# The second batch's first transform stage on pre-formed sums and differences, placed wholly ahead of the MLP

## The chip, the cores and the metric

The kernel runs on one core of a Trainium2 chip. The metric is the time of one execution in device microseconds; the table below gives it as the median of several runs. Engines are named as the profile names them: PE is TensorE (matrix products), PEld its weight loads, DVE is VectorE, ACT is ScalarE, POOL is GpSimd, SP is SyncE, which here only issues DMAs. SBUF is the on-chip working memory, PSUM the banks into which PE accumulates.

## What is computed

A Fourier filter over the sequence of 3008 tokens, then a two-layer MLP over all 24064 tokens.

```python
x: (8, 3008, 256)   w_r, w_i: (256, 256)   moe_w_in: (256, 2048)   moe_w_out: (2048, 256)

X = np.fft.rfft(x, axis=1)
Yr = Xr @ w_r - Xi @ w_i + b_r
Yi = Xr @ w_i + Xi @ w_r + b_i
Yr = np.sign(Yr) * np.maximum(np.abs(Yr) - 0.01, 0.0)      # and Yi likewise
y = np.fft.irfft(Yr + 1j * Yi, n=3008, axis=1)
...
h = y.reshape(24064, 256) @ w_in
out = np.maximum(0.01 * h, h) @ w_out
```

The MLP's weights arrive as float64 and are turned into pairs of floats (`hi` and `lo`) on the chip.

## The kernel before

**Tiling.** 3008 = 47 x 64. A batch's forward transform is a stage over 47 points (`stage_a`, with the constant matrices `fa`), a round trip of the result through HBM (`u_dram`), and a stage over 64 points (`stage_b`). Then come the products with `w_r` and `w_i` (`proj`), the threshold, the inverse stage over 64 points (`stage_g`), a second round trip (`v_dram`), and the inverse stage over 47 points (`inverse`), which makes token columns for the MLP. `fwd(b)` runs the first stage of batch b, `mid(b)` the middle ones, in 12 steps (`NPAIR`).

**The MLP** runs over 47 chunks of 512 tokens, in 8 steps each: `moe_a` and `moe_b` make the hidden layer in PSUM banks of the tag `psh` (four of them), ACT and DVE turn it into the pair `gh`, `gl`, and `moe_o` multiplies that by `w_out`.

**Batches.** Batches 0 and 1 go first: `fwd(0)`, then `mid(0)`, and inside the steps of `mid(0)` the reads of `x` for batch 1 (`fp`, lines 719 to 732). After `mid(0)` come `inverse` and `forms` for the first chunk of tokens, and the MLP starts. From there the other batches' stages are threaded through the MLP.

**First stage of batch 1** (`stage_a1`, line 273). The symmetric stage needs the sum and the difference of two halves of the input, xa and xb. For batch 0 DVE forms them (`fold`). For batch 1 nothing forms them: each of the two outputs takes two matrix products, one on xa and one on xb, so that a chunk of input costs four products instead of two; for this a third, negated matrix `fa2` is made by ACT (line 707). The input comes in seven chunks (six of 512 columns, one of 256). Five chunks run ahead of the MLP and two, numbers 4 and 5, inside its first steps (`if i in (2, 4): next(fp.gen)`), in banks of the tag `psf`.

**Order.** Instructions are put in order by a scheduler that works with the priorities in which the code is recorded; `tc.issue_after(...)` holds an instruction behind another one in that order. Each engine, and each engine's DMA queue, then runs its instructions strictly in that order, and waits on semaphores. SP issues nearly all reads, `u_dram<-xin` writes of batch 1 (line 283) and `vin<-v_dram` reads of the first inverse (line 461); ACT issues the `v_dram<-v` writes of `mid(0)` (line 420).

**Names and lines of before** that are used below: L282 ACT copies the first stage's result out of PSUM; L482 PE's products of `inverse`; L485, L486, L488, L495 the ACT and DVE work behind them; L507, L508 the casts of the token columns; L94 and L609 the products of the MLP; L133 to L139, L164 to L174, L202 to L204 the conversion of the weights; L349, L350 the two steps that make the tile `ef` of a step of `mid`; L382, L390, L391, L392 the DVE chain of one step behind `proj` (the bias, the sum, the clipping, the threshold); L396, L400 ACT's making of `zf`; L418 ACT's copy of `v`. In batches 1 to 7 L382 runs on POOL, for batch 0 on DVE.

Of the kernel before, what the change touches and what calls it, by code (L numbers as in the profile page):

```python
# [8 lines left out]
F32 = mybir.dt.float32  # L9
# [9 lines left out]
N1, N2, NK1 = 47, 64, 24  # L19
NG, NS = 5, 13  # L20
P = 128
PA = NK1 * NG
# [8 lines left out]
def spectral_mlp_kernel(  # L31
# [18 lines left out]
    D = w_r.shape[0]  # L50
# [3 lines left out]
    NPAIR = NK1 // 2  # L54
# [11 lines left out]
    sb = ctx.enter_context(tc.tile_pool(name="sb", bufs=2))  # L66
    dram = ctx.enter_context(tc.tile_pool(name="dram", bufs=2, space=bass.MemoryType.DRAM))
    ps = ctx.enter_context(tc.tile_pool(name="ps", bufs=1, space=bass.MemoryType.PSUM))
    sync, act, dve, pool = nc.sync, nc.scalar, nc.vector, nc.gpsimd

    def bank(tag, bufs):
        return ps.tile([P, 512], F32, name=tag, tag=tag, bufs=bufs)

    def products(dst, pairs):

        terms = []
        for l, r in pairs:
            terms += [(l[0], r[0]), (l[0], r[1]), (l[1], r[0])] if len(l) == 2 else [(l[0], r[0])]
        for i, (a, b) in enumerate(terms):
            last = nc.tensor.matmul(dst, a, b, start=(i == 0), stop=(i == len(terms) - 1))  # L80
        return last
# [18 lines left out]
    consts = {}  # L100
# [41 lines left out]
    made, converted, parted = [], [], []  # L142
# [67 lines left out]
    u_dram = {}  # L210
    v_dram = {}

    reads, written, turned, turning, thresholded = [], [], [], [], []
    NX = -(-NS // 2)
    XT = [("gf", 2)] + [("gl", 2)] * 2 + [("gh", 2)] * 2 + [("yc", 2)] * 2
    XT1 = [("yc", 2)] * 2 + [("gf", 2), ("gh", 2), ("yl", 2), ("yh", 2), ("gh", 2)]
# [1 line left out]
    def fwd(b):  # L218
        ud = dram.tile([2, NK1, NG * NS, D], F32, name="u_dram", tag="u_dram", bufs=NPRE + 1)
        u_dram[b] = ud  # L220
        uv = ud.rearrange("c k (g s) d -> c (k g) (s d)", g=NG)
        x_t, s_t = {}, {}

        def load(c):
            cols = slice(2 * c * D, min(2 * c + 2, NS) * D)
            n = cols.stop - cols.start
            if b < NPRE:
                tag, bufs = (XT, XT1)[b][c]
                x2 = sb.tile([PA, 2, 2 * D], F32, name="xin", tag=tag, bufs=bufs)
                x_t[c] = [x2[:, h, :n] for h in range(2)]  # L230
            else:
                x_t[c] = [
                    sb.tile([PA, 2 * D], F32, name=f"xin{h}", tag="uv"[h], bufs=3 - h)[:, :n] for h in range(2)
                ]
            for h, t in enumerate(x_t[c]):
                if b == 0:
                    (act if h else sync).dma_start(t, x[b, h, :, cols])
                else:
                    with tc.issue_after(reads[-1].ins):
                        sync.dma_start(t, x[b, h, :, cols])  # L240

        def fold(c):
            xa, xb = x_t[c]
            n = xa.shape[1]
            eng = dve
            xs = sb.tile([PA, 2 * D], F32, name="xs", tag="zf", bufs=1)[:, :n] if b else xs3[:, c % 3, :n]
            eng.tensor_add(xs, xa, xb)
            eng.tensor_sub(xa, xa, xb)
            s_t[c] = [(xs,), (xa,)] if b < NPRE else [xs, xa]

        def split(c, h):
            t = s_t[c][h]
            n = t.shape[1]
            z = sb.tile([PA, 2, 2 * D], F32R, name="xz", tag="ez"[h], bufs=1)
            xh, xl = z[:, 0, :n], z[:, 1, :n]
            dve.tensor_copy(xh, t)
            dve.tensor_sub(xl, t, xh.bitcast(F32))  # L257
            s_t[c][h] = (xh, xl)

        def stage_a(c, h):  # L260
            t = x_t[c][h]
            n = t.shape[1]
            pa = (bank("psf", 2) if b else bank("psh", 4))[:PA, :n]
            products(pa, [(consts[f"fa{h}"] if b else consts[f"fa{h}32"], s_t[c][h])])
            t = x_t[c][1 - h]
            cp = act.copy(t, pa)
            if b == 0:
                turned[:] = [cp]
            st = (act if b else sync).dma_start(uv[h, :, 2 * c * D:2 * c * D + n], t)
            if b == 0:  # L270
                written.append(st)

        def stage_a1(c):

            n = x_t[c][0].shape[1]
            pas = [(bank("psf", 2) if c in (4, 5) else bank("psh", 4))[:PA, :n] for _ in range(2)]
            for h in range(2):
                with tc.issue_after(turning[NPAIR - 2].ins):
                    products(pas[h], [
                        (consts[f"fa{h}32"], (x_t[c][0],)), (consts[f"fa{2 * h}32"], (x_t[c][1],))])  # L280
            for h in range(2):
                act.copy(x_t[c][h], pas[h])  # L282
                sync.dma_start(uv[h, :, 2 * c * D:2 * c * D + n], x_t[c][h])

        if b == 1:
            for c in range(NX):
                load(c)
                yield 0
            for c in (0, 1, 2, 3, 6, 4, 5):
                stage_a1(c)  # L290
                yield 6 * x_t[c][0].shape[1]
            return

        ahead = 2 if b >= NPRE else NX
        for c in range(ahead):
            load(c)
        yield 4 * CS if b >= NPRE else 0
        fold(0)
        if b >= NPRE:
            split(0, 0)  # L300
        yield 0
        for c in range(NX):
            for h in range(2):
                if h == 0 and c + ahead < NX:
                    load(c + ahead)
                if h == 0 and c + 1 < NX:
                    fold(c + 1)
                stage_a(c, h)
                if b >= NPRE and (c + h < NX):
                    split(c + h, 1 - h)  # L310
                yield 3 * x_t[c][h].shape[1]


    def mid(b):
        ud = u_dram[b]
        vd = dram.tile([2, NK1, NG * NS, D], F32, name="v_dram", tag="v_dram")
# [95 lines left out]
        def stage_g(j):  # L412
            pg = bank("psh", 4) if b < 1 else bank("psf", 2)
            last = products(pg, [(consts["gb" if b else "gb32"], tuple(flat(z) for z in z_t.pop(j)))])
            if b == 0:
                turning.append(last)
            v = sb.tile([P, 2, D], F32, name="v", tag="v" if b else "y")
            act.copy(flat(v), pg)  # L418
            for c in range(2):
                act.dma_start(vd[c, 2 * j:2 * j + 2, :N2, :].rearrange("k n d -> n k d"), v[c * N2:(c + 1) * N2])  # L420

        for j in range(2):
            load(j)
# [31 lines left out]
    def v_load(pi):  # L455
        vin = sb.tile([PA, 2, 2, D], F32, name="vin", tag="vin")
        (b, s, _), (b1, _, _) = pairs[pi]
        for c in range(2):
            if b == b1:
                vv = v_dram[b].rearrange("c k (g s) d -> c (k g) s d", g=NG)  # L460
                ld = sync.dma_start(vin[:, c, :, :], vv[c, :, s:s + 2, :])
                if pi < 2:
                    reads.append(ld)
                continue
            for i, (b_, s_, _) in enumerate(pairs[pi]):
                vv = v_dram[b_].rearrange("c k (g s) d -> c (k g) s d", g=NG)
                sync.dma_start(vin[:, c, i, :], vv[c, :, s_, :])
        v_t[pi] = vin
# [218 lines left out]
    fa32 = sb.tile([PA, 3, PA], F32, name="fa32", tag="xi", bufs=1)  # L687
    for h in range(2):
        sync.dma_start(fa32[:, h], fa[h])
    for h in range(3):  # L690
        consts[f"fa{h}32"] = (fa32[:, h],)
    xs3 = sb.tile([PA, 3, 2 * D], F32, name="xs3", tag="yl")
    f0 = Stream(fwd(0), FWD)
# [10 lines left out]
    win_tmp = (  # L704
        sb.tile([P, NH * NIN], F32, name="cva", tag="vin"), sb.tile([P, NH * NIN], F32, name="cvq", tag="gf"),
        sb.tile([P, 4, 2, P], F32, name="ws", tag="yh"))
    act.mul(fa32[:, 2], fa32[:, 1], -1.0)
    convert_win(0)
    with tc.issue_after(turned[0].ins):
        split_consts()  # L710
# [22 lines left out]
    m0.finish()  # L733
    with tc.issue_after(thresholded[-1].ins):
        convert_win(3)
    fp.to(0.69)
    for p in due[0]:
        v_load(p)
    for eh in range(NH):
        for p in due[0]:  # L740
            inverse(p, eh)
    for _ in forms(0):
        pass
    next(wout)
    next(wout)


    mids = [Stream(mid(b), MID + PAUSE) for b in range(1, NB)]
# [1 line left out]
    for i, pos in enumerate(moe()):  # L750
        if i % 2 == 0 and len(converted) < NQ:
            with tc.issue_after(made[0].ins), tc.issue_after(made[1].ins):
                next(wout, None)
        if i in (2, 4):
            with tc.issue_after(parted[0].ins), tc.issue_after(parted[1].ins):
                next(fp.gen)
        while cur + 1 < NB - 1 and pos >= (read[cur + 1] if cur >= 0 else 0):
            for s in streams:
                s.finish()
            cur += 1  # L760
            streams = ([Stream(fwd(cur + 1), FWD + 4 * CS)] if cur else []) + [mids[cur]]
        frac = (pos - read[cur]) / (read[cur + 1] - read[cur]) if cur + 1 < NB else 1
        if cur == 0:
            frac = max(0, frac - 0.2) * 1.25
        work = frac / 0.95 * sum(s.total for s in streams)
        with tc.issue_after(converted[-1].ins) if cur == 0 else nullcontext():
            for s in streams:
                s.to(work / s.total)
                work = max(0, work - s.total)
# [103 lines left out]
```

## Time and profile before

| | us |
|---|---|
| median of 3 runs | 2571.74 (2568.99 to 2573.2) |
| the profiled execution | 2568.88 |
| its span, first to last instruction | 2567.1 |
| busy: PE, DVE, ACT, POOL | 2527.2, 1882.8, 1677.5, 118.9 |
| end of `mid(0)` on PE (last product of `stage_g`) | about 100.5 |
| first product of the MLP | 120.17 |

The 1.8 us by which the profiled execution exceeds its span lie around the program. Times in the text are counted from the start of the span. In the profile's lists a line names the source line, the engine, the operation, the tile written and the tiles read, the shape, the count, and then busy time, the mean length of one, and the idle time before it with what ended it. A product of two fp32 operands appears as two records. A merged piece of a timeline has its start, its length, and its count.

### The profile page before, as it was taken

The numbers are of one execution on the slowest core, as the hardware profiler recorded it, in microseconds if no ns is written. First come the engines' busy times: TensorE is split into PE (matmuls) and PEld (weight loads), VectorE is DVE, ScalarE is ACT, GpSimd is POOL, SyncE is SP. The second block draws the span as 40 slices with busy tenths as digits, with TensorE's granted clock in tenths as the row PEclk, the third lists the DMA queues.
The fourth block names the chain that finished last, engine by engine and source line by source line (L and its number), as shares of the span: only waits on it lengthen the run. The fifth ranks groups of instructions, "written<-read, shape, count | busy, mean of one in ns | idle before, by whom it ended". The sixth has DMA issues, their size and how long they took to land.

```text
span 2567.1 us, 42449 instructions
## 1 busy us (share of the span) xinstructions
PE 2527.2 (98%) x16204; PEld 2269.8 (88%) x16204; DVE 1882.8 (73%) x3460; ACT 1677.5 (65%) x3151; POOL 118.9 (5%) x96
## 2 busy tenths in 40 slices
PE   6999999999999999999999999999999999999999
PEld 4689888999899998999989999899998998999998
DVE  7787777777877778777787677867768777666665
ACT  4776666677566765677666676567665676655564
POOL 0001000000000000000000000000000000000000
PEclk8999999999999999999999999999999999999999
DMA  8631133111321113111141111412114111100000
GB/s 267 176 93 50 42 91 88 41 50 45 103 67 46 50 37 112 59 49 49 42 113 53 50 49 38 120 54 58 34 38 132 46 54 41 44 21 29 9 17 17
DMA packets 119904, 165.12 MB, mean 64 GB/s; under 512 B 13597, under 2 KB 69909, under 8 KB 119701
## 3 DMA queue, kind: packets, MB, share of 16 engines
q1 hardware_dynamic: 79112, 115.54, 14.7%
q10 hardware_dynamic: 40589, 46.87, 7.1%
q8 instruction: 128, 2.10, 0.4%
q14 instruction: 75, 0.61, 0.1%
HBM read 86.60 MB, written 75.76 MB: 63 GB/s over the span
## 4 chain that ended last, share of the span: by engine, by line
PE 89%; DMA 4%; DVE 3%; ACT 2%; issue 1%; ACTq 0%; SPq 0%; DVEq 0%
PE pso L609 38%; PE psh L94 34%; PE psf L80 11%; PE psf L482 3%; PE psf L345 3%; DMA xin<-x_dram 1%; DMA u_dram<-xin 1%; PE psh L80 1%; DVE gl L562 1%; DMA v_dram<-v 0%; DMA u<-u_dram 0%; DVE xz L257 0%; DVE gf L593 0%; ACT zf L400 0%; DMA vin<-v_dram 0%
## 5 line engine op out<-in xcount | busy, mean ns | idle before, releaser
L94 PE MATMUL psh<-yh,win_hi 128*128 128x256 f32 (+1 forms) x2608 | 741.3, 285 | 2.1 <-DVE gf L593 2.0
L94 PE MATMUL psh<-yl,win_hi 128*128 128x256 f32 (+1 forms) x2608 | 732.3, 281 | 0.0
L94 PE MATMUL psh<-yh,win_lo 128*128 128x256 f32 (+1 forms) x2608 | 729.6, 281 | 0.0
L562 DVE TENSOR_TENSOR gl<-gf,gh 128x1024 fp32r<-128x1024 f32 x376 | 461.0, 1226 | 309.8 <-ACT gh L560 305.9
L609 PE MATMUL pso<-gl,wout_hi 128*128 128x512 f32 x1504 | 591.6, 393 | 1.1 <-DVE gl L562 1.1
L609 PE MATMUL pso<-gh,wout_hi 128*128 128x512 f32 x1504 | 591.1, 393 | 1.0 <-ACT gh L560 1.0
L609 PE MATMUL pso<-gh,wout_lo 128*128 128x512 f32 x1504 | 589.6, 392 | 0.0
L94 PEld LDWEIGHTS psh<-yh,win_hi 128*128 128x128 f32 x2608 | 489.9, 188 | 19.7 <-DVE gf L593 4.9
L94 PEld LDWEIGHTS psh<-yl,win_hi 128*128 128x128 f32 x2608 | 490.4, 188 | 17.4 <-issue 0.5
L94 PEld LDWEIGHTS psh<-yh,win_lo 128*128 128x128 f32 x2608 | 489.0, 188 | 2.1
L560 ACT CAST gh<-gf 128x1024 fp32r<-128x1024 f32 x376 | 395.3, 1051 | 44.4 <-PE pso L609 34.9
L596 ACT ACTIVATE gf<-gf 128x768 f32<-128x768 f32 x368 | 311.7, 847 | 150.4 <-DVE gf L593 139.4
L609 PEld LDWEIGHTS pso<-gl,wout_hi 128*128 128x128 f32 x1504 | 282.5, 188 | 61.4 <-DVE gl L562 2.9
L609 PEld LDWEIGHTS pso<-gh,wout_hi 128*128 128x128 f32 x1504 | 282.8, 188 | 47.3 <-ACT gh L560 1.8
L609 PEld LDWEIGHTS pso<-gh,wout_lo 128*128 128x128 f32 x1504 | 282.5, 188 | 46.5 <-issue 0.2
L595 ACT ACTIVATE gf<-psh 128x256 f32<-128x256 f32 x368 | 142.0, 386 | 239.1 <-PE psh L94 232.0
L593 DVE TENSOR_TENSOR gf<-psh,u 128x512 f32<-128x512 f32 x368 | 252.4, 686 | 34.4 <-PE psh L94 30.7
L577 ACT COPY p<-psh 128x256 f32<-128x256 f32 x368 | 137.0, 372 | 158.0 <-PE psh L94 149.6
L382 POOL TENSOR_TENSOR kb<-bias,kc 128x512 f32<-128x512 f32 x84 | 116.3, 1385 | 2074.3 <-ACT kc L380 1877.0
L578 DVE TENSOR_TENSOR u<-psh,p 128x256 f32<-128x256 f32 x368 | 154.6, 420 | 73.8 <-ACT p L577 72.6
L580 DVE TENSOR_TENSOR gf<-psh,u 128x256 f32<-128x256 f32 x368 | 154.8, 421 | 31.1 <-PE psh L94 17.2
L581 DVE TENSOR_TENSOR gf<-psh,gf 128x256 f32<-128x256 f32 x368 | 154.5, 420 | 5.5
(128 smaller groups left out, 3173.0 us busy)
## 6 DMA issues: line engine op xcount, KB each, us to landing
u<-u_dram SPq DMA_DIRECT2D x192, 128.0 KB, 2.8
v_dram<-v ACTq DMA_DIRECT2D x192, 128.0 KB, 2.4
out_dram<-ob SPq DMA_DIRECT2D x94, 256.0 KB, 2.0
vin<-v_dram SPq DMA_DIRECT2D x96, 240.0 KB, 3.6
xin<-x_dram SPq DMA_DIRECT2D x90, 240.0 KB, 3.0
u_dram<-xin ACTq DMA_DIRECT2D x72, 240.0 KB, 2.4
u_dram<-xin SPq DMA_DIRECT2D x24, 240.0 KB, 4.4
raw<-w_out_dram SPq DMA_DIRECT2D x8, 512.0 KB, 5.3
```

The lines of the kernel that those rows point to most:

```text
L80: last = nc.tensor.matmul(dst, a, b, start=(i == 0), stop=(i == len(terms) - 1))
L94: mlp[:] = [nc.tensor.matmul(dst, a, b, start=start and i == 0, stop=i == 2, skip_group_check=True)]
L560: cp = act.copy(gh, g)
L562: parted[:] = [cp, dve.tensor_sub(gl, g, gh.bitcast(F32))]
L577: act.copy(p1, b1[:, lo])
L578: dve.tensor_add(u2, b1[:, hi], p1)
L580: dve.tensor_add(g[:, 3], b2[:, hi], u2)
L581: dve.tensor_add(g[:, 3], b2[:, lo], g[:, 3])
L593: dve.tensor_add(g[:, 1:3], b2.rearrange("p (k n) -> p k n", k=2), u2.unsqueeze(1).broadcast_to([P, 2, HT]))
L595: act.activation(g[:, 0], b1[:, lo], AF.Prelu, alpha=SLOPE)
L596: act.activation(g[:, 1:4], g[:, 1:4], AF.Prelu, alpha=SLOPE)
L609: mlp[:] = [nc.tensor.matmul(po, a[:, f, s], r[:, i], start=(f == 0 and j == 0), stop=(f == NF - 1 and j == 2),)]
```

## The change

POOL now forms sum and difference of each chunk of batch 1 as soon as it is read (`fold1`): an add into a scratch tile, a subtraction in place, and a copy of the sum over xb. The scratch tile has one buffer, under the tag `t`, and the last `v` tile of `mid(0)` takes the same buffer. `stage_a1` then needs one product for each output, and the matrix `fa2` and its ACT instruction go. All seven chunks run ahead of the MLP: five ahead of the first `inverse`, the others between the first `inverse` calls. The reads of `v_dram` are put ahead of the writes of `u_dram` in SP's queue, and the conversion of the first two pieces of `w_out` is held behind the last `v_dram` write.

```diff
+        def fold1(c):
+
+            xa, xb = x_t[c]
+            t = sb.tile([PA, 2 * D], F32, name="xs", tag="t", bufs=1)[:, :xa.shape[1]]
+            pool.tensor_add(t, xa, xb)
+            pool.tensor_sub(xa, xa, xb)
+            pool.tensor_copy(xb, t)
+
...
-            pas = [(bank("psf", 2) if c in (4, 5) else bank("psh", 4))[:PA, :n] for _ in range(2)]
+            pas = [bank("psh", 4)[:PA, :n] for _ in range(2)]
             for h in range(2):
                 with tc.issue_after(turning[NPAIR - 2].ins):
-                    products(pas[h], [
-                        (consts[f"fa{h}32"], (x_t[c][0],)), (consts[f"fa{2 * h}32"], (x_t[c][1],))])
+                    filled[:] = [products(pas[h], [(consts[f"fa{h}32"], (x_t[c][1 - h],))])]
             for h in range(2):
                 act.copy(x_t[c][h], pas[h])
-                sync.dma_start(uv[h, :, 2 * c * D:2 * c * D + n], x_t[c][h])
+                with tc.issue_after(reads[-1].ins):
+                    sync.dma_start(uv[h, :, 2 * c * D:2 * c * D + n], x_t[c][h])
...
             for c in range(NX):
                 load(c)
+                fold1(c)
                 yield 0
-            for c in (0, 1, 2, 3, 6, 4, 5):
+            for c in range(NX):
                 stage_a1(c)
-                yield 6 * x_t[c][0].shape[1]
+                yield 0
...
-            v = sb.tile([P, 2, D], F32, name="v", tag="v" if b else "y")
+            v = sb.tile([P, 2, D], F32, name="v", tag="v" if b else "y") if b or j < NPAIR - 1 else sb.tile(
+                [P, 2, D], F32, name="v", tag="t", bufs=1)
...
-    act.mul(fa32[:, 2], fa32[:, 1], -1.0)
...
-    fp.to(0.69)
     for p in due[0]:
         v_load(p)
+    for _ in range(NX - 2):
+        next(fp.gen)
+    last = filled[0]
     for eh in range(NH):
         for p in due[0]:
-            inverse(p, eh)
+            with tc.issue_after(last.ins):
+                inverse(p, eh)
+            next(fp.gen, None)
     for _ in forms(0):
         pass
-    next(wout)
-    next(wout)
+    with tc.issue_after(returned[0].ins):
+        next(wout)
+        next(wout)
...
-        if i in (2, 4):
-            with tc.issue_after(parted[0].ins), tc.issue_after(parted[1].ins):
-                next(fp.gen)
```

On POOL, during `mid(0)`, there stood nothing between the zeroing of two tiles and the first bias sum of batch 1; `xs` is the scratch tile and `xin` a chunk of input, and after the change 21 instructions stand there, of which the first six are shown:

```order
L328 MEMSET zero 48x256 x2
L246 ISA
L246 TENSOR_TENSOR xs<-xin 120x512
L247 TENSOR_TENSOR xin<-xin 120x512
L248 COPY xin<-xs 120x512
L246 TENSOR_TENSOR xs<-xin 120x512
L247 TENSOR_TENSOR xin<-xin 120x512
L248 COPY xin<-xs 120x512
```

Each waits for the one before it on POOL. On PE, between the last product of `stage_g` (`psh<-zf`) and the first of the MLP (`psh<-yh`), the pieces of the first stage (`psh<-xin`) and of `inverse` (`psf<-ga,vin`) stood and stand so:

```order
 L80 MATMUL psh<-zf,w_105 128x512 x3
-L80 MATMUL psh<-xin,fa_66 120x512 x12
-L482 MATMUL psf<-ga,vin 128x128 x4
-L80 MATMUL psh<-xin,fa_66 120x512 x4
+L80 MATMUL psh<-xin,fa_66 120x512 x10
+L494 MATMUL psf<-ga,vin 128x128 x6
+L80 MATMUL psh<-xin,fa_66 120x512 x2
+L494 MATMUL psf<-ga,vin 128x128 x2
 L80 MATMUL psh<-xin,fa_66 120x256 x2
-L482 MATMUL psf<-ga,vin 128x128 x3
-L80 MATMUL psh<-xin,fa_66 120x256 x2
-L482 MATMUL psf<-ga,vin 128x128 x9
```

Sixteen products of 512 columns and four of 256 have become twelve and two there, and the eight of chunks 4 and 5 no longer stand in the MLP. On ACT, the end of the same stretch, from a first-stage copy of 256 columns (`xin<-psh`) to the MLP's first activation, stood and stands so (first before, then after the change):

```order
L282 COPY xin<-psh 120x256 x2
L485 COPY odd<-psf 128x240
L495 COPY yc<-y 128x42
L507 CAST yh<-yc 128x512
L495 COPY yc<-y 128x428
```

```order
L289 COPY xin<-psh 120x512 x2
L497 COPY odd<-psf 128x240
L289 COPY xin<-psh 120x256 x2
L202 CAST wout_hi<-cva 128x512
L507 COPY yc<-y 128x42
L507 COPY yc<-y 128x428
L497 COPY odd<-psf 128x240
L519 CAST yh<-yc 128x512
```

The copies of all seven chunks (14 instead of 10) and a cast of `w_out` now stand ahead of the first cast of token columns (`yh`).

More of the change, by code (lines that the diff above doesn't have):

```diff
@@ L211, in spectral_mlp_kernel @@
     v_dram = {}
-    reads, written, turned, turning, thresholded = [], [], [], [], []
+    reads, written, turned, turning, thresholded, filled, returned = [], [], [], [], [], [], []
     NX = -(-NS // 2)
@@ L416, in stage_g @@
                 turning.append(last)
-            v = sb.tile([P, 2, D], F32, name="v", tag="v" if b else "y")
+            v = sb.tile([P, 2, D], F32, name="v", tag="v" if b else "y") if b or j < NPAIR - 1 else sb.tile(
+                [P, 2, D], F32, name="v", tag="t", bufs=1)
             act.copy(flat(v), pg)
             for c in range(2):
-                act.dma_start(vd[c, 2 * j:2 * j + 2, :N2, :].rearrange("k n d -> n k d"), v[c * N2:(c + 1) * N2])
+                put = act.dma_start(vd[c, 2 * j:2 * j + 2, :N2, :].rearrange("k n d -> n k d"), v[c * N2:(c + 1) * N2])
+                if b == 0:
+                    returned[:] = [put]
         for j in range(2):
@@ L689, in spectral_mlp_kernel @@
         sync.dma_start(fa32[:, h], fa[h])
-    for h in range(3):
+    for h in range(2):
         consts[f"fa{h}32"] = (fa32[:, h],)
```

## The prediction

> **What bounds the kernel now.** I read the page first, then the busy time by stretches, since the shares are averages over unlike stages.
>
> ```profile
> PE 2527.2 (98%) x16204; PEld 2269.8 (88%) x16204; DVE 1882.8 (73%) x3460; ACT 1677.5 (65%) x3151; POOL 118.9 (5%) x96
> 65.20:86.40 21.20, 20.21 (x96) 15.67 (x97) 15.42 (x28) 17.88 (x34) 0.00 (x0) 1.00 0.74 203
> 86.40:98.10 11.70, 10.24 (x46) 7.45 (x44) 7.97 (x15) 8.87 (x18) 0.00 (x0) 1.00 0.29 67
> 101.40:124.40 23.00, 22.55 (x84) 13.00 (x83) 18.68 (x36) 15.44 (x32) 0.00 (x0) 1.00 0.83 250
> 120.10:170.00 49.90, 49.90 (x224) 38.70 (x224) 42.09 (x74) 36.56 (x67) 0.00 (x0) 1.00 0.36 108
> ```
>
> In a stretch's row stand its length, then the busy time of PE, PEld, DVE, ACT and POOL, the granted PE clock, and the DMA share with GB/s. From 120 us on PE has no gap, at full clock, so a product taken out of the MLP gives its whole time. Between the end of `mid(0)` and the MLP (101.4 to 124.4) PE is nearly full too, but DVE has 18.68 of 23.00 us and ACT 15.44. In `mid(0)` PE, ACT and DVE share the work (20.21, 17.88 and 15.42 of 21.20), in a chain from engine to engine. POOL is empty until then: what it is given there lies beside the others, unless it slows them.
>
> **PE's part.** The records of the first stage of batch 1, in PE's timeline (start, length, count) and by tile:
>
> ```profile
> L80 PE MATMUL psh<-xin,fa x40: 379/592/594, 100.5 to 117.3; 120*120 120x512 f32 x32, 120*120 120x256 f32 x8
> L80 PE MATMUL psf<-xin,fa x16: 590/592/594, 121.7 to 144.3; 120*120 120x512 f32 x16
> 100.54 10.46 PE L80 MATMUL psh<-xin,fa 120*120 120x512 f32 x24
> 111.74 4.46 PE L80 MATMUL psh<-xin,fa 120*120 120x512 f32 x12
> 121.66 3.60 PE L80 MATMUL psf<-xin,fa 120*120 120x512 f32 x8
> 124.69 0.80 PE L94 MATMUL psh<-yh,win_hi 128*128 128x512 f32 x1
> 137.14 1.88 PE L80 MATMUL psf<-xin,fa 120*120 120x512 f32 x4
> 143.00 1.88 PE L80 MATMUL psf<-xin,fa 120*120 120x512 f32 x4
> ```
>
> Twenty-four records take 10.46 us, of which the last has 0.59 (a modelled end): 9.87 / 23 = 0.43 us from one record of 512 columns to the next, and 0.86 for a product of two records. All 48 + 8 records make 24 x 0.86 + 4 x 0.43 = 22.4 us. Half of that, 11.2 us, goes. Three pieces must be told apart. The two at 137.14 and 143.00 lie inside the full MLP: 4 x 0.86 = **3.4 us** gained. The piece at 121.66 (3.4 us) and half of the products ahead of 120 (4.3 us) lie where the MLP's first chunk is still being made; there PE gains 7.7 us of room, but the stage ends sooner only as far as ACT and DVE let it.
>
> **ACT's part of that stage.** These are ACT's groups that wait there, or are added to, from 102.0 to 124.5.
>
> ```profile
> L282 ACT COPY xin<-psh 120x512 f32<-120x512 f32 x8 | 4.6, 586 | 2.4 <-PE psh L80 2.4
> L282 ACT COPY xin<-psh 120x256 f32<-120x256 f32 x2 | 0.7, 372 | 1.3 <-PE psh L80 1.2
> L495 ACT COPY yc<-y 128x470 f32<-128x470 f32 x2 | 1.2, 584 | 1.7 <-ACT odd L485 0.9 <-DVE y L488 0.8
> L133 ACT ACTIVATE cvq<-raw 128x512 f32<-128x512 uint32 x1 | 0.7, 673 | 0.0
> L173 ACT CAST win_hi<-cva 128x256 fp32r<-128x256 f32 x1 | 0.4, 401 | 0.0
> ```
>
> ACT is busy 15.44 of 23.00 us and waits 7.6, of which 3.7 on PE's first stage (2.4 and 1.3). The change puts in 4 more copies (4 x 0.59 = 2.4), two L133 conversions that stood in `mid(0)` before (2 x 0.67 = 1.3; there they ran while the queue was issuing DMAs, so `mid(0)` gains nothing) and one cast of 256 columns (0.4): 4.1 us. The floor is thus 19.5 us, 3.5 earlier than 23.0; if every present wait stayed, the stage would end 4.1 later. The waits on PE mostly go, since its products are half as long; the waits along the chain product, `odd`, sum, `yc`, cast stay in part, because that chain still closes the stage, and the reads of `vin` still start behind the last `v_dram` write and the last conversion of `w_in`. I take about 1.8, half of the floor. **First-stage gain: 3.4 + 1.8 = 5.2 us**, bounds -0.7 and 6.9.
>
> **POOL's part, and whom it slows.** POOL's only two-input work of this size so far is L382, and by chance it meets DVE:
>
> ```profile
> 189.16 1.29 POOL L382 TENSOR_TENSOR kb<-bias,kc 128x512 f32<-128x512 f32 x1 [11.76 <-DVE y L488]
> 189.32 1.42 DVE L527 TENSOR_TENSOR yt<-yc,yt 128x256 f32<-128x256 f32 x1
> 188.99 0.41 DVE L578 TENSOR_TENSOR u<-psh,p 128x256 f32<-128x256 f32 x1
> 1121.75 1.65 POOL L382 TENSOR_TENSOR kb<-bias,kc 128x512 f32<-128x512 f32 x1 [25.12 <-DVE yl L508]
> 1121.56 0.68 DVE L508 TENSOR_TENSOR yl<-yt,yh 128x512 fp32r<-128x512 f32 x1
> 1122.16 1.78 DVE L508 TENSOR_TENSOR yl<-yc,yh 128x512 fp32r<-128x512 f32 x1
> ```
>
> Undisturbed, a POOL sum takes 1.29 us. A DVE operation of 256 columns with both inputs in SBUF that starts under it takes 1.42 us instead of some 0.42: it ends 0.29 us behind POOL's end. At 1121.56 it goes in turn: DVE's running operation ends at 1122.24, POOL's (1.65 long) at 1123.40, so POOL had the port for 1.16 us, and DVE's next one, begun at 1122.16, ends at 1123.94. So a DVE operation with two SBUF inputs and one on POOL exclude each other, and they take turns. DVE operations with an input in PSUM are not held.
>
> This agrees with the Trainium skill, "SBUF — State Buffer", section "Who interferes with whom", which calls the shared port pair an exclusive lock; it adds that DVE's `tensor_scalar` in a 2-port mode is held as well, which no row here shows. By that rule the five L391 below would wait too, some 3 us more, and the sum would come out at 2574.5.
>
> When does POOL run? SP's issues of the reads of `x`, DVE's groups from 65.2 to 86.4, and the nearest row for a one-input operation of POOL:
>
> ```profile
> 56.56 2.53 SPq L240 DMA_DIRECT2D xin<-x_dram  x2
> 77.29 1.31 SPq L240 DMA_DIRECT2D xin<-x_dram  x2
> xin<-x_dram SPq DMA_DIRECT2D x10, 240.0 KB, 5.2
> L319 POOL MEMSET zero<- 48x256 f32 x8 | 2.4, 306 | 0.6 <-POOLq L860 0.3
> L392 DVE TENSOR_TENSOR t<-t,c 128x512 f32<-128x512 f32 x5 | 3.5, 693 | 0.2
> L390 DVE TENSOR_TENSOR t<-psf,kb 128x512 f32<-128x512 f32 x5 | 3.4, 689 | 0.3 <-PE psf L80 0.2
> L382 DVE TENSOR_TENSOR kb<-bias,pso 128x512 f32<-128x512 f32 x4 | 2.7, 684 | 0.9 <-PE pso L80 0.9
> L391 DVE TENSOR_SCALAR c<-t 128x512 f32<-128x512 f32 x5 | 2.1, 424 | 0.1
> L350 DVE TENSOR_TENSOR ef<-ef 128x256 f32<-128x256 f32 x5 | 2.1, 423 | 4.2 <-ACT ef L349 4.2
> L174 DVE TENSOR_TENSOR win_lo<-ws,win_hi 128x1024 fp32r<-128x1024 f32 x1 | 1.2, 1225 | 0.0
> L174 DVE TENSOR_TENSOR win_lo<-cva,win_hi 128x512 fp32r<-128x512 f32 x1 | 0.7, 693 | 0.8 <-ACT win_hi L173 0.8
> L174 DVE TENSOR_TENSOR win_lo<-cva,win_hi 128x256 fp32r<-128x256 f32 x1 | 0.4, 419 | 0.0
> L170 DVE TENSOR_TENSOR ws<-cva,ws 128x256 f32<-128x256 f32 x1 | 0.4, 418 | 0.0
> ```
>
> The second chunk's reads go out at 56.6 to 59.1 and land some 5 us after their issue, about 64 to 65; the last at 77.3 to 78.6, landing about 81 to 83. POOL works from about 59 (the first chunk was issued ahead of these; I count it as hidden) to somewhere near 88. The copy on POOL is not in the trace; between 0.31 (a write of half its width) and 1.29 (a sum of its width) I take 0.6, twice the nearest row. The port time from the second chunk on: 10 full sums and differences x 1.16, 5 copies x 0.5, and 1.4 for the short chunk: 15.5 us.
>
> DVE is busy 15.42 of the 21.20 us of that stretch, so it has 5.8 us to spare. If the whole 15.5 us fell on DVE, it would end 9.7 us late. If POOL always found DVE idle or reading PSUM (5.8 + 3.4 + 2.7 us, 2.1 more under L391), nothing would be late. Counted by turns: fourteen DVE operations there have two SBUF inputs (L392 and L350 five each, L174 three, L170 one). Those that follow another held one find POOL just begun and wait 1.16; those behind L382 and L390 (1.4 us together) find it part done. At two thirds, 0.77 us, fourteen waits are 10.8 us, less 5.8 to spare: **5.0 us** late, bounds 0 and 9.7. Behind DVE wait L392's readers (`zf` on ACT, then `stage_g` on PE), and the rest of `mid(0)` shifts as a whole, since from 86.4 on its steps follow each other closely (DVE 7.97 of 11.70, PE 10.24).
>
> **The rest costs nothing.** The last `v` on the tag `t` waits for POOL's last copy; that is some 10 us ahead of the end of `stage_g` at 100.5, where that tile is needed. The writes of `u_dram` leave SP later ahead of the MLP, but chunks 4 and 5, whose products ran at 121.66 to 143.00, now leave ahead of it. Two reads of `w_out` wait in SP behind all these writes and go out near 118 instead of 109.9; ACT's conversion of them stood at 124.31. They land in about 7 us, so a wait of a microsecond is possible in front of the first activation; PE has four banks to fill meanwhile.
>
> ```profile
> 124.31 0.67 ACT L133 ACTIVATE cvq<-raw 128x512 f32<-128x512 uint32 x1
> 109.89 1.02 SPq L188 DMA_DIRECT2D raw<-w_out_dram  x2
> raw<-w_out_dram SPq DMA_DIRECT2D x2, 512.0 KB, 7.2
> ```
>
> **The sum.** 2568.88 - 5.2 + 5.0 = 2568.7 for the profiled execution. That one lies 2.86 below the median of the three runs, so on the median's scale 2571.5.
>
> **Rivals.**
> - *POOL fits into the gaps, and ACT's waits go.* POOL's operations fall under PSUM reads and DMA waits (cost 0.5) and the stage closes near ACT's floor (gain 6.9): 2571.74 - 6.9 + 0.5 = 2565.3. For it: 5.8 us of DVE idle and 6.1 of PSUM reads. Against: 14 held operations in a row with little between.
> - *DVE becomes the bound of `mid(0)`* (slower). Nearly each POOL operation holds DVE for its length: 9.7 us, while only the MLP's 3.4 us and little more come back: 2571.74 + 9.7 - 3.4 = 2578.0. It decides from an average wait of (5.8 + 5.2) / 14 = 0.79 us up, only just above my 0.77; a copy of 1.2 us or a held L391 pushes there.
> - *The first stage does not end sooner.* ACT's waits stay, so that the MLP starts as late as before: only 3.4 is gained against 5.0: 2573.3. Speaks for it: the stage's closing chain is unchanged.
>
> **How the numbers follow.** A measurement of this kernel tells about 0.2% (5 us) from no change. My forecast, 2571.5, 0.50; the first rival 0.24; the second 0.18; the third 0.08. The first is faster by over 0.2%, the second slower, the forecast and the third within: 0.24, 0.58, 0.18. The range reaches nearly to the rivals, 2565.5 to 2577.0: the gain's upper end with half of the cost gives 2567, the full cost with the gain as taken 2576.2.
>
> **What would show it.** Right: DVE's L350, L392 and L174 lengthened to 1 to 2 us between 60 and 90 us; the last product of `stage_g` near 105; from there 17 to 19 us to the MLP's first product instead of 19.6; no first stage in the MLP. Wrong on POOL: those groups at their old means and `stage_g` ending at 100.5. Wrong on ACT: ACT's idle time between the copies as large as before. It would be wrong altogether if POOL ended behind 101 us, so that the last `v` waited for it, or if the MLP showed new gaps from late `w_out`.

## The result and the profile after

| | median us | runs | ratio to before, 95% interval |
|---|---|---|---|
| before, same chip | 2570.98 | 9 | |
| after | 2578.42 (2575.72 to 2581.04) | 9 | 1.0036 [1.0027, 1.0044] |

The change made the kernel 7.4 us slower by the medians. The prediction was 2571.5, and the time lies above its range, which ended at 2577.0. The profiled execution of after took 2581.04 us (span 2578.2), the slowest of the nine, so its trace holds some losses that the median does not. The ratios here and below come from the single runs and not from the two medians, whose quotient (1.0029 here) can differ from them by up to 0.07%.

The page's first part, and the busy time by stretches of the kernel after (length, then PE, PEld, DVE, ACT and POOL, granted PE clock, DMA share and GB/s); the first two stretches have the same times as those shown of before, the others are moved with the end of `mid(0)` and the start of the MLP:

```profile
PE 2523.0 (98%) x16176; PEld 2267.9 (88%) x16176; DVE 1891.5 (73%) x3460; ACT 1675.6 (65%) x3150; POOL 142.4 (6%) x117
65.20:86.40 21.20, 15.02 (x71) 11.29 (x72) 20.52 (x24) 14.66 (x28) 17.23 (x14) 1.00 0.72 210
86.40:98.10 11.70, 10.41 (x50) 8.08 (x50) 7.48 (x13) 6.77 (x15) 3.66 (x5) 1.00 0.23 53
107.10:130.10 23.00, 17.75 (x68) 9.61 (x66) 19.58 (x37) 16.80 (x37) 0.00 (x0) 1.00 0.72 220
130.10:180.00 49.90, 49.68 (x240) 41.27 (x241) 42.34 (x74) 34.88 (x62) 0.00 (x0) 0.97 0.38 108
```

PE has 28 records fewer, as forecast (14 products of two records). But between 65 and 86 DVE is busy 20.52 of 21.20 us with 24 instructions, where before it was busy 15.42 with 28, and PE fell from 20.21 to 15.02. In the stretch ahead of the MLP PE has 17.75 of 23.00 us, where it had 22.55. And in the MLP's first 50 us the granted clock is 0.97 and no longer 1.00.

**First, mid(0).** GpSimd's groups, and DVE's largest, held or not, from 60 us to 92 (after):

```profile
L246 POOL TENSOR_TENSOR xs<-xin 120x512 f32<-120x512 f32 x6 | 9.8, 1639 | 62.6 <-DMA xin<-x_dram 62.3
L247 POOL TENSOR_TENSOR xin<-xin 120x512 f32<-120x512 f32 x6 | 9.0, 1503 | 0.5
L248 POOL COPY xin<-xs 120x512 f32<-120x512 f32 x6 | 4.3, 719 | 0.4
L401 DVE TENSOR_TENSOR t<-t,c 128x512 f32<-128x512 f32 x5 | 6.0, 1209 | 0.1
L359 DVE TENSOR_TENSOR ef<-ef 128x256 f32<-128x256 f32 x5 | 4.6, 927 | 1.1 <-ACT ef L358 1.1
L399 DVE TENSOR_TENSOR t<-psf,kb 128x512 f32<-128x512 f32 x6 | 4.1, 685 | 0.2
L391 DVE TENSOR_TENSOR kb<-bias,pso 128x512 f32<-128x512 f32 x6 | 4.1, 676 | 0.0
L400 DVE TENSOR_SCALAR c<-t 128x512 f32<-128x512 f32 x5 | 3.7, 748 | 0.1
```

L401 (L392 before) went from a mean of 692 ns to 1209, L359 (L350) from 423 to 927, and the `tensor_scalar` L400 (L391) from 424 to 748. L399 and L391, with an input in PSUM, stayed at 685 and 676. So what waits is what the prediction named, the DVE operations with two SBUF inputs, and the `tensor_scalar` with them. Against e2 below, which has the same order on DVE, 15 operations of DVE are held, for 10.2 us in all. GpSimd pays as well: its sums take 1.64 us on average instead of 1.29.

The chain's end on PE tells what it costs. The first `stage_b` products and the last two of `stage_g`, before and then after:

```profile
35.47 5.46 PE L345 MATMUL psh<-fb,u 128*128 128x128 f32 x24 [9.06 <-DMA u<-u_dram]
99.61 1.10 PE L80 MATMUL psh<-zf,w 128*128 128x512 f32 x2 [1.01 <-ACT zf L396]
```

```profile
37.86 5.11 PE L354 MATMUL psh<-fb,u 128*128 128x128 f32 x24 [11.47 <-ACT cva L134]
106.12 1.12 PE L80 MATMUL psh<-zf,w 128*128 128x512 f32 x2 [0.96 <-ACT zf L405]
```

`mid(0)` took 64.1 us from the start of the one to the start of the other before, and 68.3 after. The 2.4 us by which it began later are not the change's: in the kernels below that start lies anywhere from 35.4 to 38.4, also with the same instructions ahead of it (e7 and e11).

**Second, the start of the MLP.** SP's queue, the chain of waits, ACT and PE at that place (after), one line or two of each:

```profile
116.13 11.14 SPq L291 DMA_DIRECT2D u_dram<-xin  x14
127.36 0.92 SPq L188 DMA_DIRECT2D raw<-w_out_dram  x2
```

```profile
124.46 4.52 DMA u_dram<-xin
```

```profile
129.06 0.93 ACT L519 CAST yh<-yc 128x256 fp32r<-128x256 f32 x2 [2.11 <-DMA u_dram<-xin]
130.03 0.50 PE L94 MATMUL psh<-yh,win_hi 128*128 128x512 f32 x1 [2.44 <-ACT yh L519]
```

All 14 writes of `u_dram` now stand behind the reads of `v_dram`. Chunk 5 lies in a buffer of the tag `yh`, its write is issued at 124.46 and lands 4.52 us later, and ACT's cast into that buffer waits 2.11 us for it; PE stands for 2.44. Behind this gap the clock is granted at half (after; the gap, then the stretch behind it):

```profile
127.60:130.03 2.43, 0.00 (x0) 0.00 (x0) 0.51 (x3) 0.97 (x3) 0.00 (x0) 1.00 0.90 208
131.20:134.60 3.40, 3.40 (x10) 2.41 (x9) 1.45 (x4) 1.71 (x3) 0.00 (x0) 0.50 1.00 263
```

**Third, inside the MLP.** PE's gaps between 300 and 380 us, before and then after:

```profile
306.56 0.39 PE L80 MATMUL psf<-wr_hi,eh 128*128 128x256 f32 x1 [1.46 <-ACT eh L360]
362.16 0.50 PE L80 MATMUL psf<-xz,fa_hi 120*120 120x512 f32 x1 [0.93 <-DVE xz L256]
363.51 1.00 PE L80 MATMUL psf<-xz,fa_hi 120*120 120x512 f32 x2 [0.86 <-DVE xz L256]
```

```profile
311.88 0.62 PE L621 MATMUL pso<-gh,wout_hi 128*128 128x512 f32 x1 [2.81 <-ACT ob L626]
369.64 1.72 PE L80 MATMUL psf<-xz,fa_hi 120*120 120x512 f32 x3 [2.33 <-DVE xz L264]
377.00 1.63 PE L80 MATMUL psf<-xz,fa_hi 120*120 120x512 f32 x2 [2.87 <-DVE xz L264]
```

3.3 us became 8.0, at instructions that the diff does not touch. Each of the three gaps of after is followed by 3.4 us at half clock, at 312, 370 and 377 us, where before has one such stretch, behind its pair. Two of them as stretches, before and then after:

```profile
365.10:368.50 3.40, 3.34 (x11) 2.46 (x11) 2.52 (x5) 1.54 (x4) 0.00 (x0) 0.50 0.57 157
```

```profile
312.10:315.50 3.40, 3.40 (x9) 2.62 (x9) 1.64 (x4) 2.30 (x5) 0.00 (x0) 0.50 0.20 77
```

The scheduler sets the order of the whole program, and with fewer products in the MLP's first steps it put another order on PE from there on; the two sequences of PE are the same again from 413.2 us in before and 422.6 in after. For instance, the three products `psf<-zh` ahead of batch 2's first stage stood among twelve of `pso<-gh` and `pso<-gl` before, and stand among the next 21 of `psh` after, close ahead of `psf<-xz`. Which of these shifts makes which gap was not taken apart.

Set against before, the trace of after is 2.4 us late at the start, 4.1 more at the end of `mid(0)`, 2.8 more from there to the place where the two sequences meet again, and 2.3 more at the end, of which a half-clock stretch at 2162 makes 1.7 if it costs half its length: 11.6 in all. The third of these should have been shorter by the first-stage gain. Instead, from the MLP's first product to that place, PE stands for 11.5 us, all gaps counted, where it stood for 3.7, and has half clock for 13.7 us, where it had it for 3.4.

The output stores of the MLP are poor marks inside that stretch. The third was issued 137.4 us behind the end of `mid(0)` before and 132.9 after, 4.5 sooner. But from the MLP's first product to that store PE had 673 records before and 644 after. Of the 29, 16 are the first stage's; 13 were only put behind the store, which at some 0.21 us each (49.68 us for 240 records in the stretch above) is 2.7 of the 4.5 us, an estimate.

### The profile page after: what moved, and what is told of

It reads as the page before. It is cut to its first block, busy times and chain, and to the rows that moved or that the text cites. A ratio compares the mean times of both kernels' runs of the same rounds, so it can differ in the third digit from the quotient of the medians.

```text
span 2578.2 us, 42446 instructions
## 1 busy us (share of the span) xinstructions
PE 2523.0 (98%) x16176; PEld 2267.9 (88%) x16176; DVE 1891.5 (73%) x3460; ACT 1675.6 (65%) x3150; POOL 142.4 (6%) x117
## 4 chain that ended last, share of the span: by engine, by line
PE 90%; DMA 3%; DVE 3%; ACT 2%; issue 1%; SPq 1%; ACTq 0%; DVEq 0%
PE pso L621 39%; PE psh L94 35%; PE psf L80 11%; PE psf L494 3%; PE psf L354 3%; DMA xin<-x_dram 1%; DMA u_dram<-xin 1%; DVE gl L574 0%; DMA v_dram<-v 0%; PE psh L80 0%; DMA u<-u_dram 0%; DMA vin<-v_dram 0%; DVE t L401 0%; DMA raw<-w_out_dram 0%; SPq L340 0%
## 5 line engine op out<-in xcount | busy, mean ns | idle before, releaser
L391 POOL TENSOR_TENSOR kb<-bias,kc 128x512 f32<-128x512 f32 x84 | 114.4, 1362 | 1998.6 <-ACT kc L389 1837.0
```

## The experiments

Theory A: GpSimd holds DVE at the port. B: the new order alone. C: the late writes hold the buffer of `yh`. D: the order inside the MLP. Ratios are to the kernel before, in runs on the same chip; 0.1% is 2.6 us. "mid" is the length of `mid(0)` as above, "to store 3" the time from its end to the issue of the third output store, "to same order" the time from its end to the record of the MLP from which PE's sequence is the same in all these kernels (e8 excepted), "gaps" PE's gaps above 0.25 us between 140 and 390 us. The last four columns are of one profiled execution each.

| kernel | median us | ratio, 95% interval | mid | to store 3 | to same order | gaps |
|---|---|---|---|---|---|---|
| before (trace) | | | 64.1 | 137.4 | 313.6 | 3.3 |
| after (trace) | 2578.42 | 1.0036 [1.0027, 1.0044] | 68.3 | 132.9 | 316.5 | 8.0 |
| e1 | 2574.82 | 1.0028 [1.0016, 1.0039] | 70.1 | 139.1 | 316.8 | 3.6 |
| e2 | 2573.13 | 1.0014 [1.0005, 1.0023] | 62.7 | 132.9 | 316.9 | 8.4 |
| e3 | 2581.56 | 1.0044 [1.0031, 1.0057] | 68.2 | 132.9 | 315.1 | 8.5 |
| e4 | 2576.74 | 1.0037 [1.0024, 1.0051] | 67.5 | 129.8 | 313.2 | 8.0 |
| e5 | 2575.11 | 1.0021 [1.0012, 1.0029] | 68.2 | 133.2 | 314.0 | 5.4 |
| e6 | 2571.32 | 1.0008 [0.9999, 1.0017] | 64.6 | 134.8 | 315.3 | 5.9 |
| e7 | 2574.61 | 1.0017 [1.0008, 1.0026] | 68.4 | 129.9 | 311.2 | 5.1 |
| e8 | 2581.77 | 1.0049 [1.0033, 1.0065] | 72.7 | 138.1 |  | 4.9 |
| e9 | 2572.12 | 1.0008 [1.0000, 1.0017] | 64.1 | 134.6 | 314.5 | 4.7 |
| e10 | 2575.08 | 1.0024 [1.0015, 1.0034] | 68.5 | 133.2 | 314.1 | 4.7 |
| e11 | 2573.24 | 1.0013 [1.0004, 1.0021] | 67.4 | 130.4 | 310.2 | 5.0 |
| e12 | 2571.37 | 1.0004 [0.9995, 1.0013] | 64.7 | 133.1 | 313.9 | 5.2 |
| e13 | 2566.20 | 0.9996 [0.9987, 1.0005] | 62.8 | 130.9 | 310.2 | 4.7 |
| e14 | 2574.54 | 1.0022 [1.0012, 1.0033] | 62.3 | 135.4 | 320.9 | 6.9 |
| e15 | 2579.85 | 1.0040 [1.0028, 1.0053] | 68.8 | 131.5 | 315.0 | 7.2 |

**e1 and e2: GpSimd's operations alone.** They differ from before and from after in nothing but GpSimd's queue.

```diff
 e1, on before
             for c in range(NX):
                 load(c)
+                fold1(c)
                 yield 0
...
+            pool.tensor_add(t, xa, xb)
+            pool.tensor_sub(t, xa, xb)
+            pool.tensor_copy(t, xa)
...
 e2, on after
-                fold1(c)
```

> The kernel before, with the 21 GpSimd operations added in mid(0) on a scratch tile and their results unused; the order on PE, DVE, ACT and SP is that of before. Theory A (DVE is held by GpSimd at the shared port): stage_g ends some 5 us later than before's 100.5, L350, L392 and L174 lengthen, and the time is 2571.0 + 5 = 2576. Theory B (the loss lies in the new order, not in GpSimd): stage_g ends where it did and the time is 2571.0.

> The changed kernel without its 21 GpSimd operations: the first stage of batch 1 then runs on the raw halves xa and xb, so the sums and differences are left out of the result; the order on PE, DVE, ACT and SP is that of the changed kernel. Theory A: 5 us less than the changed kernel, 2573.4. Theory B (new order alone): 2578.4, as the changed kernel. If both hold a part, what is left above 2571.0 is the price of the new order, net of the 3.4 us of saved products.

The first `stage_b` products and the last of `stage_g` in e1, then two of DVE's groups and the same products in e2:

```profile
37.41 5.39 PE L354 MATMUL psh<-fb,u 128*128 128x128 f32 x24 [10.92 <-DMA u<-u_dram]
107.52 2.04 PE L80 MATMUL psh<-zf,w 128*128 128x512 f32 x2 [1.01 <-ACT zf L405]
```

```profile
L400 DVE TENSOR_TENSOR t<-t,c 128x512 f32<-128x512 f32 x7 | 4.8, 690 | 0.2
L399 DVE TENSOR_SCALAR c<-t 128x512 f32<-128x512 f32 x7 | 3.0, 425 | 0.1
36.70 4.41 PE L353 MATMUL psh<-fb,u 128*128 128x128 f32 x24 [10.39 <-ACT cvq L133]
99.44 1.10 PE L80 MATMUL psh<-zf,w 128*128 128x512 f32 x2 [1.09 <-DVE zf L406]
```

Without GpSimd's work the DVE groups are back at 690 and 425 ns. The work costs `mid(0)` 6.0 us in the old order (70.1 less 64.1) and 5.5 in the new one (68.3 less 62.7), and the time 0.28% and 0.22% by the ratios, 7 and 6 us. The 6.0 may hold a little more than the port: in e1's trace PE has half clock for 6.83 us from 69.9, inside `mid(0)`, which the trace of before has not. A third pair below with one order, e11 and e13, gives 4.6 (67.4 less 62.8). Theory A holds, and its size was nearly right. But e2 is still 0.14% slower than before, with 28 records of PE less to do and `mid(0)` 1.4 us shorter (62.7): B holds a part too.

**e3 and e4: the writes of `u_dram`.**

```diff
 e3, on after
-    for p in due[0]:
-        v_load(p)
     for _ in range(NX - 2):
         next(fp.gen)
+    for p in due[0]:
+        v_load(p)
...
-                with tc.issue_after(reads[-1].ins):
-                    sync.dma_start(uv[h, :, 2 * c * D:2 * c * D + n], x_t[c][h])
+                sync.dma_start(uv[h, :, 2 * c * D:2 * c * D + n], x_t[c][h])
 e4, on after
-            for c in range(NX):
+            for c in (0, 1, 5, 4, 2, 3, 6):
                 stage_a1(c)
```

> The changed kernel with the first reads of v_dram recorded behind the first five chunks again, and the u_dram writes no longer held behind them, so that SP's queue is mixed as before and two w_out reads go out ahead of the last eight writes. Theory C (late u_dram writes keep the buffer of the tile yh, and late w_out reads stop ACT): the 2.4 us gap of PE at 127.6 and the two waits of ACT of 1.3 us go, the time is 2.5 us less, 2576. If these waits are hidden: 2578.4, with GpSimd's part still in it. If the reads of v_dram are later by what stands ahead of them: up to 2 us more.

> The changed kernel with the first stage of batch 1 in the order of chunks 0, 1, 5, 4, 2, 3, 6, so that the chunk in the buffers of yh is written out third and not sixth; SP's queue is the same row by row. Theory C: only the wait of ACT for the buffer of yh goes, PE's gap of 2.4 us at 127.6 goes with it, and the time is 2576.2; the waits for w_out stay. If another wait ends there just as late: 2578.4.

In e3 the MLP's first product came 1.8 us later behind `mid(0)` than in after (20.6 and 18.9 us behind the start of the last `stage_g` pair), and PE's gaps above 0.25 us from there to 140 us shrank only from 3.1 us to 2.3: the last of the three cases expected. That gap of 2.3 us now waits for a read of `v_dram`, and ACT's cast into `yh` still waits 1.62 us for a write of `u_dram`. What the earlier writes and w_out reads won, the later reads of `v_dram` lost. In e4 PE's long wait is gone:

```profile
126.60 0.50 PE L94 MATMUL psh<-yh,win_hi 128*128 128x512 f32 x1 [0.36 <-ACT yh L519]
126.10:129.50 3.40, 2.81 (x10) 1.70 (x10) 1.86 (x3) 1.41 (x3) 0.00 (x0) 1.00 0.82 226
```

0.36 us in place of 2.44, the clock at 1.00, and store 3 comes 3.1 us earlier, the place of the same order 3.3. The ratio shows none of this against after's, which comes from another group of runs; the intervals are 2 us (after) and 3.5 us (e4) to each side, so a gain of 3 could just hide in them.

**e5, e6, e7: the order in the MLP.** One number of the pacing moves the start of batch 1's middle stages a little and so makes the scheduler find another order. Nothing ahead of the MLP changes by it.

```diff
 e5, on after; with the chunk order of e4 it is e7
-            frac = max(0, frac - 0.2) * 1.25
+            frac = max(0, frac - 0.19) / (1 - 0.19)
 e6, on before: the same line, and fold1 of the change for two chunks
+                if c in (4, 5):
+                    fold1(c)
...
+                    products(pas[h], [(consts[f"fa{h}32"], (x_t[c][1 - h],))] if c in (4, 5) else [
```

> The changed kernel with one number of the MLP's pacing altered (batch 1's middle stages start at 0.19 instead of 0.2 of their stretch); by the scheduler's order this brings the instructions around the start of batch 2's first stage back to the sequence that the kernel before has there, and alters nothing ahead of the MLP. Theory D (the rest of the loss is an accident of the scheduler's new order inside the MLP): the three gaps of PE at 309, 367 and 374 us (8.0 us) shrink to before's 3.3, two of the half-clock pulses of 3.4 us behind them go (1.7 us each), and the time falls by about 8 us to 2570. Rival (the gaps only show a delay that sits elsewhere, as in the late w_out reads): the gaps move and the time stays at 2578.

> The kernel before, where GpSimd folds only chunks 4 and 5, whose first stage stays inside the MLP's first steps, one product for each output; the MLP's pacing as in e5. Four products of 0.86 us go from the full MLP: 3.4 us. Theory A: six GpSimd operations of 21 hold DVE for 2/7 of 6 us, 1.7. Together 1.7 us less than before, 2567 to 2569. If only the last chunks' operations meet a busy DVE, or if the order in the MLP is not that of before in effect, it comes out at before's time or up to 5 us above.

> e5 with the chunk order of e4 (0, 1, 5, 4, 2, 3, 6). Theory C: PE's gap of 2.4 us at 127.6 and the half-clock pulse at 131 go as well, 3.8 us less than e5: 2566 to 2567, the fastest of all. If e4 had no effect on the time because the MLP makes it up elsewhere: as e5, 2570.

PE's gaps in e5 at the places of the three:

```profile
311.54 0.50 PE L80 MATMUL psf<-zh,gb_hi 128*128 128x512 f32 x1 [2.46 <-ACT zh L416]
368.38 0.49 PE L80 MATMUL psf<-xz,fa_hi 120*120 120x512 f32 x1 [0.93 <-DVE xz L264]
369.73 1.28 PE L80 MATMUL psf<-xz,fa_hi 120*120 120x512 f32 x2 [0.87 <-DVE xz L264]
```

The two gaps at batch 2's first stage fell to 0.93 and 0.87 us (before: 0.93 and 0.86). The one at 309 stayed, now ahead of another product. e5 lies 0.15% (4 us) below after's ratio, half of what was forecast, as about half of the gaps' growth went. e6 missed: it is not faster than before. GpSimd's six operations cost `mid(0)` 0.4 us, less than thought, and four products are gone from the MLP, but the gap of 2.46 us at 306 and its half-clock stretch are there as well, another such stretch lies at 100, and the place of the same order comes 1.7 us later than in before. (Store 3 comes 2.6 us earlier, but as in after 13 records that stood ahead of it stand behind it.) e7 lies 0.04% below e5, where its trace has 3.4 us less to store 3 and 2.8 to the same order.

**e8: the sums on DVE.** In place of GpSimd, on e7:

```diff
+            dve.tensor_add(xa, xa, xb)
+            dve.scalar_tensor_tensor(xb, xb, -2.0, xa, ALU.mult, ALU.add)
...
```

> e7 with the sums and differences formed by DVE instead of GpSimd, two operations a chunk in place (xa + xb, then that less twice xb), 14 operations of at most 0.69 us, 9.3 us in mid(0). If the shared port is handed over whole (theory A), GpSimd's 21 operations cost DVE as much as doing the work itself, and mid(0) ends as late as in the changed kernel, 5 to 7 us behind before's 100.5. If GpSimd's hold is partial, DVE's own work is the dearer way: mid(0) ends 8 to 10 us late.

```profile
L245 DVE TENSOR_TENSOR xin<-xin 120x512 f32<-120x512 f32 x6 | 4.1, 687 | 4.5 <-DMA xin<-x_dram 4.3
L246 DVE SCALAR_TENSOR_TENSOR xin<-xin 120x512 f32<-120x512 f32 x6 | 4.1, 684 | 0.0
```

`mid(0)` took 72.7 us, 8.5 above before and 4.2 above e7. So GpSimd's hold is partial: 4.6 to 6.0 us of `mid(0)` for 25 us of GpSimd's work, where DVE itself, in 9.0 us, cost 8.5. (The order differs from e7's in `mid(0)` and the MLP too, so the time is not compared.)

**e9 to e12: one order for all.** At a pace of 0.23 the scheduler gives before, after, after with e4's chunk order, and two folded chunks the same sequence of products from 243 to 246 us on, past batch 2's first stage.

```diff
+            frac = max(0, frac - 0.23) / (1 - 0.23)
 e12 beside it, on before: chunks 4 and 5 only, the sum in a third slice of their tile
+                x2 = sb.tile([PA, 3 if c in (4, 5) and b else 2, 2 * D], F32, name="xin", tag=tag, bufs=bufs)
...
+            pool.tensor_add(s_t[c], xa, xb)
+            pool.tensor_sub(xa, xa, xb)
```

> The kernel before with batch 1's middle stages started at 0.23 instead of 0.2 of their stretch: at this pace the scheduler gives all four kernels of this group the same order of products from 250 us to the start of batch 2's first stage, so that they can be compared without the accident of the order. It is the group's own base. Theory D: within 0.1% of the kernel before, as long as the new sequence has no gap above 2 us; if it has one, up to 5 us more.

> The changed kernel at the same pace of 0.23. From the profiles so far: GpSimd's hold +5.5, the w_out conversion moved out of mid(0) -1.4, from the end of mid(0) to the third output store -4.5, together about 0 against e9, and up to +2 with the half-clock pulse behind PE's wait at 127. Theory D (a good part of the 7.4 us was the order): so 0 to 2 us above e9. If order plays no part: 7 to 9 us above e9.

> e10 with the chunk order 0, 1, 5, 4, 2, 3, 6. Theory C: PE's wait at 127 shrinks by 2.1 us and its half-clock pulse goes, 2 to 4 us below e10, so some 2 us below e9. If nothing comes of it, as e10.

> e9 where GpSimd folds chunks 4 and 5 only, in two operations each (the sum goes to a third slice of the chunk's own tile, so that no copy is needed), and their first stage takes one product for each output, still inside the MLP. Saved: 4 products of 0.86, 3.4 us; held: 4 of GpSimd's 21 operations, 4 x 0.27 = 1.1 us by e2, 0.9 by e6's profile with six. So 2 to 3 us below e9, the fastest of the group beside e11. If the MLP's full stretch does not give the product time back: as e9.

With nearly the same gaps (4.7 to 5.2 us) the change costs 3.0 us by the medians (e10 less e9; 4.1 by the ratios), where it cost 7.4 as it came (9.3). That is more than the 0 to 2 expected, and the expectation shows why: it took 4.5 us of gain up to store 3. In one order the gain is 0.4 us (314.5 less 314.1), with the wait on `yh` in it, and 4.3 in e11 without that wait (314.5 less 310.2). By the medians e4's chunk order takes only 1.8 off, and e11's interval still overlaps e10's; e11 lies above e9, not 2 below it. e12 is 0.8 below e9, less than the 2 to 3 expected, and not told apart from it or from before.

**e13 to e15: does it close, and is the order still the price?** e13 is e11 without `fold1`; e14 is e12, and e15 is e11, at a pace of 0.18.

> e11 without its 21 GpSimd operations: the first stage of batch 1 runs on the raw halves, the sums and differences are left out of the result; the order on the other four engines is that of e11. If the three costs close the sum: e11 less 5.5 us, about 0.2% below e11 and 0.08% below the kernel before (2567 to 2568). If something else of the change still costs: e11's time less 2 or nothing.

> e12 at a pace of 0.18. mid(0) 0.5 us longer than before's, four products of 0.86 us less in the MLP; if the order at 0.18 has gaps no larger than before's (3.3 us in all from 140 to 390): 2 to 3 us below the kernel before, the only one of these that would be faster. If its order has a gap above 2 us with its half-clock stretch: as e6, 2 us above.

> e11 at a pace of 0.18: mid(0) 4 us longer than before's, from there to the third output store some 7 us less. If the order at 0.18 is as good as before's: 0 to 3 us below the kernel before. If it has a gap above 2 us: as e7, 4 us above.

e13 is the fastest: 0.17% (4.4 us) below e11 by the ratios, with an interval that takes in the kernel before, and with `mid(0)` 4.6 us shorter. It leaves the sums out, so it is no candidate. e14 and e15 show the order's price from the other side; a gap of each:

```profile
249.03 0.50 PE L80 MATMUL psf<-zh,gb_hi 128*128 128x512 f32 x1 [2.54 <-ACT zh L417]
```

```profile
250.93 0.50 PE L80 MATMUL psf<-zh,gb_hi 128*128 128x512 f32 x1 [2.54 <-ACT zh L416]
```

Each has two gaps of 2.5 us, at 250 and near 310, with half-clock stretches behind three of the four. The pace alone takes e12 from 1.0004 to 1.0022, and e11 from 1.0013 to 1.0040: 5.7 and 10 us above before, where 2 and 4 were expected for an order with such a gap. No version that computes the reference was faster than before.

## Why the prediction was wrong

**GpSimd and DVE: right, in mechanism and size.** 5.0 us was forecast, 5.5 (after against e2), 6.0 (e1 against before) and 4.6 (e11 against e13) were measured. The count by turns was near as well: fourteen waits of 0.77 us, 10.8 in all, against fifteen in after, 10.2 in all. It left L400 out (L391 before). It was held too, as the rule from the Trainium skill, "SBUF — State Buffer", section "Who interferes with whom", says of `tensor_scalar` in a 2-port mode: 748 ns instead of 424. By that rule the prediction's sum was 2574.5, with 3 us for L400 (five waits of its own 0.77 us would have been 3.9); its five operations waited 5 x 0.32 = 1.6 us.

**The move of the w_out conversion: a small miss.** `mid(0)` was said to gain nothing by it. e2 has it 1.4 us shorter than before. Whether that is the conversion itself was not tried apart.

**The first-stage gain: right only without the wait on `yh`.** 5.2 us was forecast. In one order e11 gains 4.3 against e9 from the end of `mid(0)` on, and e10, with the wait, 0.4. That after's third store came 4.5 us sooner looks like the forecast, but is luck: 13 records had been put behind that store. The MLP's first product came 1.7 us sooner behind the end of `mid(0)`, near the 1.8 taken. (The 4.3 us that the prediction calls half of the products ahead of 120 are that half, 7.7, less the 3.4 of the four products that move there from the MLP; its sum of 7.7 us of room stands.)

**"The rest costs nothing": this is the step that failed,** at two places. The late `u_dram` writes were looked at only for who reads them, and the w_out reads behind them. They also set free the buffers in which the chunks lie, and the MLP's `yh` is such a buffer: 2.4 us of PE and a half-clock stretch, 3.8 us in the traces of one order (e10 less e11), 1.8 by their medians. And the MLP was taken as full ("a product taken out of the MLP gives its whole time"). It is full only in the order that it has. In the new order three gaps of 8.0 us stand where 3.3 stood, with more half-clock time behind them. Given one order (e9 and e10), the change costs 3.0 us by the medians and not 7.4, 4.1 and not 9.3 by the ratios. Of these 5.1 us by the ratios, 3.1 are the order of after (0.36% less 0.24%, whose intervals still overlap), and 2.1 come from the common order, which is worse for before itself. That the order alone moves the time by such amounts is shown by e12 and e14, and by e11 and e15, which differ in the pace only. Beside GpSimd's hold the order is the largest part.

**The second rival gave 2578.0, almost the measured time, for another reason.** Its hold of 9.7 us did not come; 5.5 did, and the wait on `yh` and the order made up the rest. That its number fits is luck. Its condition, DVE as the bound of `mid(0)`, was met between 65 and 86 us (20.52 of 21.20), but not further.

**What stays open.** The traces give e4's chunk order some 3 us each time (3.3, 2.8 and 3.8 to the same order for e4, e7 and e11 against after, e5 and e10), the medians 0.5 and 1.8 for e7 and e11. Half-clock stretches that come in some executions only may hide the rest; that was not settled. Nor is it shown which of the scheduler's shifts makes which gap.

## What to carry to other kernels

Where a scheduler sets one order for the whole program, a product saved early can be paid for later in an order that nobody chose: compare the kernels' order beyond the place of the edit, and test the edit at one or two other paces before judging it. Work given to an idle GpSimd beside a DVE that reads two SBUF inputs is paid for by DVE, here 4.6 to 6.0 us for 25 us of it; that is cheaper than the 8.5 us that DVE's own work cost, but not free. A mark inside a program, such as an output store, measures a gain only if the same work stands ahead of it in both kernels. A DMA write that is moved later keeps its source buffer longer, so look up which later tile takes that buffer.

## What the runs showed of the hardware

Gaps of PE far shorter than 3.4 us are followed by half-clock stretches. Inside the MLP these last 3.41 us in the profiles here, or twice or three times that. They follow 21 of the 24 gaps of 2.3 to 2.9 us between 120 and 390 us, and every pair of about 0.93 and 0.87 us at batch 2's first stage; a single one of 1.46 us at 305 (before) had none. The Trainium skill, "TensorE: Matmul & The Clock Gate", section "HAM oscillation — how this bites in real kernels", gives its rule as no idle gaps above about 3.4 us; these traces don't agree, since each of the three gaps in after is below that. As an estimate, a gap of 2.5 us on a full PE should here be counted at 2.5 plus half of 3.4. GpSimd's copy of 120x512 between SBUF tiles takes 0.72 us on average (0.6 was assumed), less than half of its sum of the same width (1.64).
